# Batch 0 loaded nine rows to a partition, and weights in rows of 4 KB: a change to the start of an attention and FFN kernel

## The chip, the cores and the metric

The kernel runs on one core of a Trainium2 chip. TensorE (PE) multiplies; its weight loads (PEld) run beside its matmuls. VectorE (DVE), ScalarE (ACT) and GpSimd (POOL) work on elements. SyncE (SP) does no arithmetic here: its queue issues the DMA transfers, which 16 DMA engines carry out. The metric is the device time of one execution in microseconds; less is better.

## The reference

There are 8 batches of 8 heads, 576 rows and 64 columns a head. Only the largest scores of a row count, those within tau of its maximum; then a bilinear FFN follows.

```python
scores = scale * np.matmul(q, k.transpose(0, 1, 3, 2))
thresh = np.max(scores, axis=-1, keepdims=True) - tau
scores = np.where(scores >= thresh, scores, -1000000000.0)
scores = scores - np.max(scores, axis=-1, keepdims=True)
attn = np.exp(scores)
attn = attn / (np.sum(attn, axis=-1, keepdims=True) + 1e-09)
attn_out = np.matmul(attn, v)                 # (8, 8, 576, 64)
x = attn_out.transpose(0, 2, 1, 3).reshape(4608, 512)
out = ((x @ w_a) * (x @ w_b)) @ w_out         # w_a, w_b: 512x1536, w_out: 1536x512
```

q, k, v are float32. The three weights arrive as float64, so an element has 8 bytes; 512 x 1536 of them are 6.3 MB. The order of the keys within a head does not matter to the result as long as k and v have the same one; the order of the queries decides only which row of the output a result belongs to.

## The kernel before, in words

**Units and slots.** Two heads make a pair (index `i`, four pairs a batch). A unit `(i, u)` is 128 query rows of both heads of a pair (64 and 64 on the partitions), or the 64 rows that remain of two pairs. The main loop over `g` (L1000) takes one unit a slot and interleaves several stages: the scores of unit `g` on PE (L397, 16 recorded matmuls), its row maxima on DVE (L404), exponential on ACT (L425), threshold and row sums on DVE (L428), then the turned weights of earlier units times v (`product`, L535, tile pv). Matmuls are 64x64 and use the four quarters of the array side by side.

**Two ways to turn.** The first eight units (`BY_PE`) turn their attention weights on PE, by a product with a diagonal matrix (L472). Later ones are turned in blocks of 32 by DVE (L491), written to DRAM (`swap`, L497) and read back (`wT`, L514); for these, v has to lie in an order that fits the blocks. That is why `load_v` is called again for batch 0 in slots 8 to 11 (L1099).

**First rows.** q and k of batch 0 are loaded straight into "rooms" (L197): parts of tiles that are not yet in use, 96 partitions, six rows of 64 elements on each. `prep_pe` (L366) transposes them on PE, six transposes of 96 rows a matrix; `prep_copy` (L381) copies the result to SBUF on DVE, or ACT for the first k (L978). Pair 0 is prepared ahead of the loop, pair `g`+1 in slot `g`: q after the scores, k near the slot's end.

**Weights.** 36 pieces of [128, 512] are loaded by `load_weights` (L253) as raw float64 and made float32 by integer arithmetic: ACT takes the two halves of each number (L297, L298), POOL clamps (L304), DVE sets the sign and shifts (L310, L318), POOL adds (L323). A slot converts two pieces, slots 4 to 9 three. `load_weights` is called in four places of a slot and loads at most one piece at each, if a raw buffer or one of the idle tiles in `extra` is free; an issue then waits for the last PE instruction recorded ahead of it. Pieces 0 to 23 are w_a and w_b in turn, by column group of 512 columns: each is two transfers of 64 partitions with two runs of 2 KB. Pieces 24 to 35 are w_out, one transfer of 512 KB in runs of 4 KB.

**The FFN as a filler.** `ffn` is a generator of PE steps; `advance` (L910) takes steps out of it at several places of a slot until the columns owed are worked off. A step that is not ready (weights not converted, or rows of x not there) yields 0, and the advance is over. The first block (256 rows of batch 0) starts while weights are still being converted: six column blocks `f`, two to a column group, with 128 rows at a time for the first four of them (L758), then 256 rows. By the end of slot 4 the first 128 rows of x are there, by slot 9 all 256.

**Queues.** All instructions of an engine keep the order in which they are recorded. SP's transfers do too, and each waits for the completion of the transfer issued eight before it. PSUM is four double banks, shared by scores, transposes, pv, and the FFN.

Of the kernel before, what the change touches and what calls it, by code (L numbers as in the profile page):

```python
# [54 lines left out]
def kernel(  # L55
# [50 lines left out]
    R = 96  # L106
    NR = S // R
# [84 lines left out]
    def load_rows(i, name, room, engine=nc.sync):  # L192

        b, hp = pairs[i]
        for j in range(2):
            rows = {"q": q, "k": k}[name][b, 2 * hp + j]
            engine.dma_start(room[:, :, j * D:(j + 1) * D], rows.rearrange("(n p) d -> p n d", p=R))  # L197
        loaded.setdefault(i, {})[name] = room

    def load_v(i, again=False):  # L200
# [3 lines left out]
        for j in range(2):  # L204
            rows, half = v[b, 2 * hp + j], loaded[i]["v"][j * D:(j + 1) * D]
            if i >= HP or again:
                if i < HP:
                    rows = rows.rearrange("(c s p) d -> p c s d", c=2, p=Q)
                else:
                    rows = rows.rearrange("(p c s) d -> p c s d", c=2, p=Q)  # L210
                post(("v", i), *((half[c * Q:(c + 1) * Q], rows[:, c]) for c in range(2)))
            else:
                nc.sync.dma_start(half, rows.rearrange("(s p) d -> p s d", p=D))
# [11 lines left out]
    for f in range(NG):  # L225
        for c in range(HP):
            for dst, w in ((wa_sb, w_a), (wb_sb, w_b)):
                src = []
                for r in range(2):
                    chunks = [(2 * c + e) % HP * 2 + (r + (c >= HP // 2)) % 2 for e in range(2)]  # L230
                    cols = slice(f * CW + r * CH, f * CW + (r + 1) * CH)
                    rows = w[:, cols].bitcast(U32).rearrange("(k p) f -> p k f", p=D)
                    src.append(rows[:, chunks[0]:chunks[1] + 1:2])
                pieces.append((dst[:, f, 2 * c:2 * c + 2].rearrange("p k f -> p (k f)"), src))
    for F in range(NF):
        pieces.append((wo_sb[:, F, :], [w_out[F * P:(F + 1) * P, :].bitcast(U32)]))
# [42 lines left out]
    def convert_first(n):  # L279
# [17 lines left out]
        nc.scalar.activation(top, raw[:, :, 1].bitcast(FP32), AF.Abs)  # L297
# [22 lines left out]
    def convert_add(n):  # L320
        if n in stages:
            top, low = pieces[n][0].bitcast(I32), stages.pop(n).bitcast(I32)
# [6 lines left out]
    ROWS = 2 * NR * D  # L329
    rooms = []  # L330
    for _ in range(TW_BUFS):
        t = work.tile([P, 2 * NB, Q], FP32, tag="tw", bufs=TW_BUFS, name="rows")
        rooms.append(t.rearrange("p n e -> p (n e)")[0:R, 0:ROWS])
    rooms += [sums_sb[0:R, c:c + ROWS] for c in range(0, 5 * ROWS, ROWS)]
    rooms = [t.rearrange("p (n w) -> p n w", n=NR) for t in rooms]
# [30 lines left out]
    def prep_pe(i, name):  # L366

        m = loaded[i][name]
        if name == "q":
            mT = first_sb[:, i * S:(i + 1) * S]  # L370
        else:
# [788 lines left out]
```

## Time and profile before

| | |
|---|---|
| median of 3 runs | 1430.45 us (1425.97 to 1431.11) |
| the profiled execution | 1424.12 us, its span 1422.3 us |
| PE busy | 1370.2 us (96%) |
| DVE, ACT, POOL busy | 1005.4, 679.4, 480.9 us |
| DMA | 223.25 MB, 327003 packets, 171536 of them under 512 B |
| chain that ended last | PE 86%, DVE 8%, DMA 3%, issue 2% |

The span is the time from the first to the last instruction of the profiled execution; its own time is 1.8 us more. A group of instructions is given as line, engine, operation, output from input, shape and count. "Idle before" is time in which the engine stood still before the group, with what ended it; "issue" means that the profile shows nothing that it waited for. A share of the DMA engines above 1 comes from transfers that overlap in an engine. fp32 matmuls are recorded twice, transposes once.

### The profile page before, as it was taken

What the parts mean: (1) busy time and instruction counts of PE and PEld (TensorE: products, weight loads), DVE (VectorE), ACT (ScalarE), POOL (GpSimd) and SP (SyncE); (2) the same over time, 40 slices, a digit from 0 to 9 for tenths busy, and PEclk for the clock granted to TensorE, in tenths of its full rate; (3) what the DMA queues carried; (4) which work ended last, traced back from release to release, by engine and by line L of the source; (5) the groups of instructions that cost most, each with busy time, mean ns of one, the idle gap of its engine ahead of it and who ended that gap; (6) DMA issues with size and microseconds to landing.
All of it is one profiled execution on the core that took longest, in us unless ns stands there. A gap on an engine that the chain in (4) does not pass through costs nothing.

```text
span 1422.3 us, 76965 instructions
## 1 busy us (share of the span) xinstructions
PE 1370.2 (96%) x34208; PEld 1237.5 (87%) x34208; DVE 1005.4 (71%) x2196; ACT 679.4 (48%) x1244; POOL 480.9 (34%) x668
## 2 busy tenths in 40 slices
PE   6788999999999999999999999999999999999998
PEld 4677679999878897889999999988898999799998
DVE  6898876788677777786767767677767776744323
ACT  5877554545444554545444545454545545431010
POOL 2764541606060605133333324241515060605000
PEclk9989999999999999999999999999999999999999
DMA  9977786667656775667555766567655775550000
GB/s 211 235 210 202 179 218 161 178 159 194 172 144 167 190 195 147 178 160 185 143 131 151 179 178 168 138 161 212 159 145 145 209 182 152 130 151 18 3 18 17
DMA packets 327003, 223.25 MB, mean 157 GB/s; under 512 B 171536, under 2 KB 310800, under 8 KB 326672
## 3 DMA queue, kind: packets, MB, share of 16 engines
q1 hardware_dynamic: 324160, 217.74, 59.7%
q8 instruction: 269, 4.41, 1.3%
q10 hardware_dynamic: 2512, 0.59, 0.2%
q14 instruction: 62, 0.51, 0.1%
HBM read 128.58 MB, written 89.65 MB: 153 GB/s over the span
## 4 chain that ended last, share of the span: by engine, by line
PE 86%; DVE 8%; DMA 3%; issue 2%; ACT 1%; SPq 1%; DVEq 0%; ACTq 0%
PE pab L700 27%; PE po L830 20%; PE pab L773 18%; PE pv L535 10%; PE sc L397 9%; DVE mx L404 2%; DVE tw L491 1%; DVE tw L428 1%; SPq L143 1%; DMA wT<-swap 1%; DVE thr L405 1%; DVE low L310 1%; DMA more_u<-in_moe_w_a_dram 1%; PE tp L472 0%; DMA raw<-in_moe_w_b_dram 0%
## 5 line engine op out<-in xcount | busy, mean ns | idle before, releaser
L404 DVE TENSOR_REDUCE mx<-sc 128x1 f32<-128x576 f32 x288 | 204.6, 752 | 131.8 <-PE sc L397 131.4
L447 ACT ACTIVATE tw<-tw,rcp 128x576 f32<-128x576 f32 x272 | 196.1, 768 | 196.2 <-DVE rcp L441 196.1
L425 ACT ACTIVATE tw<-sc,bias,scalars 128x576 f32<-128x576 f32 x288 | 239.6, 832 | 10.9 <-PE pab L773 0.4
L666 POOL TENSOR_TENSOR h<-h,u 128x512 f32<-128x512 f32 x28 | 35.2, 1279 | 604.5 <-DVE h L743 428.0
L428 DVE SCALAR_TENSOR_TENSOR tw<-sc,thr,tw 128x576 f32<-128x576 f32 x288 | 221.2, 798 | 9.1 <-ACT tw L425 8.3
L830 PE MATMUL po<-wo_sb,h 64*64 64x256 f32 x3264 | 206.9, 376 | 1.2 <-DVE h L743 1.1
L491 DVE STREAM_TRANSPOSE tw<-tw 128x576 f32<-128x576 f32 x272 | 194.4, 752 | 0.8 <-ACT tw L447 0.8
L830 PEld LDWEIGHTS po<-wo_sb,h 64*64 64x64 f32 x3264 | 158.0, 133 | 25.6 <-DVE h L743 2.6
L535 PE MATMUL pv<-wT,vm 64*64 64x160 f32 (+3 forms) x5184 | 169.8, 273 | 7.0 <-DMA wT<-swap 2.4
L535 PEld LDWEIGHTS pv<-wT,vm 64*64 64x64 f32 x5184 | 159.3, 135 | 19.6 <-issue 9.6
L397 PE MATMUL sc<-kT,qT 64*64 64x288 f32 x2016 | 167.8, 404 | 0.6 <-DVE xT L543 0.3
L830 PE MATMUL po<-sums_u,h 64*64 64x256 f32 x2448 | 154.1, 376 | 0.5 <-DVE h L781 0.5
L799 POOL TENSOR_TENSOR h<-h 128x256 f32<-128x256 f32 x168 | 117.5, 734 | 106.5 <-PE po L830 101.7
L830 PEld LDWEIGHTS po<-sums_u,h 64*64 64x64 f32 x2448 | 117.6, 133 | 20.3 <-DVE h L781 1.6
L700 PE MATMUL pab<-xU,wb_sb 64*64 64x128 f32 x4096 | 131.6, 269 | 0.0
L700 PEld LDWEIGHTS pab<-xU,wb_sb 64*64 64x64 f32 x4096 | 126.9, 133 | 2.6 <-ACT h L725 0.5
L397 PEld LDWEIGHTS sc<-kT,qT 64*64 64x64 f32 x2016 | 102.5, 133 | 20.8 <-issue 4.6
L542 ACT COPY xT<-pv 128x128 f32<-128x128 f32 (+1 forms) x68 | 17.6, 259 | 206.5 <-PE pv L535 206.5
L424 ACT ACTIVATE bias<-mx,scalars 128x1 f32<-128x1 f32 x288 | 82.7, 287 | 68.3 <-DVE mx L404 68.0
L543 DVE COPY xT<-pv 64x128 f32<-64x128 f32 (+1 forms) x136 | 38.1, 281 | 92.3 <-PE pv L535 91.1
L773 PE MATMUL pab<-xS,wa_sb 64*64 64x256 f32 (+1 forms) x1536 | 98.8, 361 | 0.0
L773 PE MATMUL pab<-xS,wb_sb 64*64 64x256 f32 (+1 forms) x1536 | 97.0, 360 | 0.7 <-issue 0.7
(136 smaller groups left out, 2370.1 us busy)
## 6 DMA issues: line engine op xcount, KB each, us to landing
wT<-swap SPq DMA_DIRECT2D x244, 288.0 KB, 4.0
swap<-tw SPq DMA_DIRECT2D x480, 144.0 KB, 3.1
vm<-in_v_dram SPq DMA_DIRECT2D x128, 72.0 KB, 2.5
swap<-tw SPq DMA_DIRECT2D x128, 72.0 KB, 3.2
kT<-in_k_dram SPq DMA_DIRECT2D x112, 72.0 KB, 3.4
wT<-swap SPq DMA_DIRECT2D x56, 144.0 KB, 3.6
out_dram<-kept SPq DMA_DIRECT2D x30, 256.0 KB, 3.8
qT<-in_q_dram SPq DMA_DIRECT2D x112, 40.0 KB, 3.0
```

What stands on the lines that cost most here:

```text
L397: nc.tensor.matmul(sc[m][o * D:(o + 1) * D, c], qT[r, q0:q0 + D], kT[r, c * SH:(c + 1) * SH], start=True, stop=True)
L404: nc.vector.tensor_reduce(mx[:, c], sc[j], axis=AX.XY, op=ALU.max)
L424: nc.scalar.activation(bias[:, j:j + 1], mx[:, j:j + 1], AF.Copy, scale=e_nscale)
L425: nc.scalar.activation(wb[j], sb[j], AF.Exp, bias=bias[:, j:j + 1], scale=e_scale)
L428: nc.vector.scalar_tensor_tensor(out=wv, in0=sb[j], scalar=thr[:, j:j + 1], in1=wv, op0=ALU.is_ge, op1=ALU.mult, accum_out=sums[:, j:j + 1])
L447: nc.scalar.activation(w, w, AF.Copy, scale=rcp[:, j:j + 1])
L491: nc.vector.transpose(w, w)
L535: nc.tensor.matmul(pv[c * D:(c + 1) * D, y], vm[rows, s], wT[y](rows, s), start=(s == 0), stop=(s == NSLOT - 1))
L700: nc.tensor.matmul(out[c * D:(c + 1) * D, r, f * P:(f + 1) * P], w[g][k][rows, w0:w0 + D], moving[k][rows], start=(fresh and k == 0 and f ...
L773: nc.tensor.matmul(pab[c * D:(c + 1) * D, r], w[rows, f // n, k, fs + c * D:fs + (c + 1) * D], moving, start=(k == 0), stop=(k == H - 1))
L799: (nc.vector if state["over"] else nc.gpsimd).tensor_tensor(*a, **kw)
L830: nc.tensor.matmul(po[c * D:(c + 1) * D, r, y], ht[rows, t0:t0 + D], other[rows, f], start=(f == 0), stop=(f == NF // 2 - 1))
```

## The change

- q and k of batch 0: partition p of 64 takes nine rows that follow each other in DRAM (2304 B), q of a pair on the lower and k on the upper 64 partitions of one room. Keys and queries of batch 0 are thereby in another order: row 9p + n of the head is entry 64n + p.
- `prep_pe` transposes with matmuls of 64x64 against the identity, 20 a matrix (slot 4 of the nine is cut in two where a PSUM bank ends), q and k of pair 0 in one interleaved run.
- v of batch 0 is loaded in the same order, 2304 B to a partition; when it is loaded again for the blocks, in 8 transfers a pair instead of 4.
- The output rows of batch 0 are written back in their order: [2, 64 rows] instead of [128 rows] a transfer.
- Weights: column group 0 as before. Groups 1 and 2 come together: all pieces of w_a, then of w_b, each in two transfers of 64 partitions with one run of 512 columns (4 KB); half of the array's rows works on columns 512 to 1023, the other half on 1024 to 1535. The rows of w_out are permuted to fit.
- The first block therefore has 128 rows at a time only for the first two column blocks, then 256 rows: w_a for the rest, then w_b. Its steps wait for 8, 16 and 24 converted pieces.
- One of the four places of a slot that load a weight piece is gone.

```diff
@@ load_rows, load_v
-            engine.dma_start(room[:, :, j * D:(j + 1) * D], rows.rearrange("(n p) d -> p n d", p=R))
+            engine.dma_start(room[:, j], rows.rearrange("(p n) d -> p (n d)", p=D))
...
-                    rows = rows.rearrange("(c s p) d -> p c s d", c=2, p=Q)
+                    rows = rows.rearrange("(x p n) d -> p x n d", x=2, p=Q)
+                    post(("v", i), *((half[c * Q:(c + 1) * Q, y::2],
+                                      rows[:, (c + y) % 2, (c * NSLOT + y) // 2:(c * NSLOT + y) // 2 + (NSLOT + 1 - y) // 2])
+                                     for c in range(2) for y in range(2)))
...
-                nc.sync.dma_start(half, rows.rearrange("(s p) d -> p s d", p=D))
+                nc.sync.dma_start(half, rows.rearrange("(p s) d -> p s d", p=D))
@@ weight pieces
-    for f in range(NG):
-        for c in range(HP):
-            for dst, w in ((wa_sb, w_a), (wb_sb, w_b)):
...
+    for c in range(HP):
+        for dst, w in ((wa_sb, w_a), (wb_sb, w_b)):
...
+            pieces.append((dst[:, 0, 2 * c:2 * c + 2], src))
+    for dst, w in ((wa_sb, w_a), (wb_sb, w_b)):
+        for c in range(H):
+            src = []
+            for r in range(2):
+                rows = w[chunk_of(c, r) * D:(chunk_of(c, r) + 1) * D, CW + r * CW:2 * CW + r * CW]
+                src.append(rows.bitcast(U32).rearrange("p (k f) -> p k f", k=2))
+            pieces.append((dst[:, 1:NG, c], src))
     for F in range(NF):
-        pieces.append((wo_sb[:, F, :], [w_out[F * P:(F + 1) * P, :].bitcast(U32)]))
+        g, r, y = F // NT, F // 2 % 2, F % 2
+        row = (F if g == 0 else NT + r * NT + (g - 1) * 2 + y) * P
+        pieces.append((wo_sb[:, F, :].rearrange("p (k f) -> p k f", k=2), [w_out[row:row + P, :].bitcast(U32)]))
@@ prep_pe
-                nc.tensor.transpose(tp[:, c, n * R:(n + 1) * R], m[:, c * (NR // 2) + n], ident[0:R, 0:R])
...
+        for n in range(NSLOT):
+            for c0, c1 in ((0, D),) if n != NT else ((0, Q), (Q, D)):
+                c, to = divmod(n * D + c0, SH)
+                for name, (_, tp) in zip(names, both):
+                    m, r = loaded[i][name], "qk".index(name) * D
+                    for j in range(2):
+                        nc.tensor.matmul(tp[j * D:(j + 1) * D, c, to:to + c1 - c0], m[:, j, n * D:(n + 1) * D],
+                                         ident[r:r + D, r + c0:r + c1], start=True, stop=True)
@@ ffn
-            steps = [(f, c, c + P) for c in (0, P) for f in range(2 * n)] + steps[2 * n:]
+            steps = ([(f, c, c + P, both) for c in (0, P) for f in range(n)]
+                     + [(f, 0, HALF, (w,)) for w in both for f in range(n, NG * n)])
...
-                while (state["converted"] < 2 * HP * (f // n + 1)
+                while (state["converted"] < 2 * HP * (1 + (f // n > 0) * (1 + any(w is wb_sb for w in both)))
@@ rows_out
-            pending.append((out[r0:r0 + P, :], t))
+            to = out[r0:r0 + P, :]
+            if b == 0:
+                n = (h * HALF + u * P) // D
+                to = out[0:S, :].rearrange("(p n) d -> n p d", n=NSLOT)[n:n + 2]
+            pending.append((to, t))
@@ main loop
-        load_weights(RAWS, most=1)
         if here:
             weigh(i, u)
```

## The prediction

> **What bounds the kernel now.** I read the page's parts 1 and 2 first, then the busy time by stage, then the order of time on TensorE, VectorE and the DMA queue inside the stage that is not full.
>
> The stages (columns: stretch in us, its length, then PE, PEld, DVE, ACT and POOL busy us with instruction counts, granted clock, DMA share, GB/s):
>
> ```profile
> 0.00:60.00 60.00, 39.17 (x796) 31.28 (x796) 44.89 (x107) 40.39 (x83) 27.71 (x39) 0.97 1.11 225
> 60.00:100.00 40.00, 34.26 (x930) 31.93 (x934) 35.04 (x75) 32.14 (x64) 27.69 (x32) 0.87 0.72 191
> 100.00:185.00 85.00, 74.68 (x1597) 58.55 (x1593) 74.64 (x167) 54.11 (x105) 40.74 (x40) 0.96 0.78 203
> 185.00:1285.00 1100.00, 1090.55 (x27586) 987.14 (x27582) 802.81 (x1762) 537.84 (x970) 366.99 (x531) 1.00 0.64 166
> 1285.00:1422.30 137.30, 131.52 (x3322) 128.61 (x3314) 47.99 (x88) 14.94 (x24) 17.79 (x29) 0.99 0.05 15
> ```
>
> From 185 us on PE is busy 99% and 96% of the time. The instruction order of the two kernels on PE is the same from the second FFN block on, apart from a few groups of 4 matmuls that change sides of a scores group. So the change can move the end only through the first 185 us, where PE idles 20.8 + 5.7 + 10.3 = 36.9 us. The end moves with the time at which the first block is through (before: 185 us, in slot 21).
>
> In that stage the work goes slot by slot: scores, row maximum, exponential, threshold, and two or three weight pieces converted. By the starts of the row maxima a slot lasts 7.2, 7.4, 7.9, 6.6, 7.1, 9.1, 12.2, 9.3, 11.3 and 9.8 us (slots 0 to 9). DVE is busy for nearly all of a 7 us slot; ACT, with three pieces, for about 8.4 us. Slots 6 and 8 stand out. The order of time on PE, then on DVE, says why (start, duration, group; in brackets the idle time before it and what ended it):
>
> ```profile
> 5.33 2.15 PE L376 MATMUL tp<-more_u,rows 96*128 96x96 f32 x12 [5.33 <-DMA rows<-in_q_dram]
> ...
> 53.83 1.22 PE L397 MATMUL sc<-kT,first_u 64*64 64x288 f32 x15
> 58.10 0.40 PE L397 MATMUL sc<-kT,first_u 64*64 64x288 f32 x1 [3.06 <-issue]
> ...
> 60.20 3.85 PE L472 MATMUL tp<-first_u,tw 128*64 128x128 f32 x36 [0.65 <-DVE xT L543]
> ...
> 81.66 1.99 PE L773 MATMUL pab<-xT,wa_sb 64*64 64x128 f32 x32 [1.45 <-DVE tw L428]
> 83.39 1.96 PE L773 MATMUL pab<-xS,wa_sb 64*64 64x128 f32 x32
> 85.10 1.96 PE L773 MATMUL pab<-xT,wb_sb 64*64 64x128 f32 x32
> ```
>
> ```profile
> 58.54 0.76 DVE L404 TENSOR_REDUCE mx<-sc 128x1 f32<-128x576 f32 x1 [2.14 <-PE sc L397]
> ...
> 88.37 1.42 DVE L404 TENSOR_REDUCE mx<-sc 128x1 f32<-128x576 f32 x2 [2.60 <-PE sc L397]
> ```
>
> In slot 6 PE stopped for 3.06 us before the last of 16 scores matmuls with nothing that the profile shows to wait for: the instruction itself was late, while the DMA engines were full (share 1.07). The 36 matmuls after it then took 3.85 us instead of 2.19, at a granted clock of 0.66. In slot 8 a filler of 96 first-block matmuls ran at half rate (1.96 us a group instead of 1.08), the next scores stood behind it, and DVE idled 2.60 us.
>
> No converting instruction waits for a weight transfer in this stage: the waits list a DMA only for the first rows (5.3 us) and 0.2 us for v. Weights are issued early enough to hide a landing of 7 to 8 us. So faster weight transfers, by themselves, are worth nothing on the chain.
>
> **The change part by part.** Gains are negative.
>
> *First rows.* q and k of pair 0 (590 KB) go as 64 runs of 2304 B a transfer instead of 576 of 256 B. The first landing ended at 5.19. The engines moved 265 to 275 GB/s at their best between 2.5 and 4 us, and 337 from 105 to 110 us, when w_out's rows of 4 KB were in flight. 590 KB at 270 is 2.2 us, at 337 1.75. I take 0.7 us, bounds 0 and 1.5.
>
> *Transposes.* Per matrix six full-width transposes (0.71 us warm, 1.22 cold) become 20 matmuls of 64x64, which the profile will count as 40, as it counts 16 for 8 scores matmuls. The nearest row is pv with 72 such on four quarters in 1.27 us: 18 to a quarter, 70 ns each. Pair 0 uses all four quarters: 20 x 70 = 1.4 us warm, 2.1 to 2.4 at the cold rate (the first scores took 2.2 us instead of 1.2), against 2.15 before. Nothing. Pairs 1 to 3 have two quarters only: 1.07 to 1.4 warm, about 2.1 cold, so +0.4 to +0.9 each, six times. For k DVE comes 0.5 us later anyway and covers some; for q the copy is what DVE does next. I put 0.55 + 0.55 + 0.5 = +1.6 over slots 0 to 2, bounds 0 (PE idles 6 us there) and +4.
>
> A rule of the Trainium skill bears on this. TensorEngine Tiling (Array Packing), "Restrictions", says that column tiling rules out the transpose mode for FP32 input; TensorE: Matmul & The Clock Gate calls that mode four times as fast for FP32 under "Terms". By the rule a matrix would take 4 x 0.71 / 2 = 1.4 us, the upper of my two warm values, and the term would be near +2.5.
>
> *Slot 6.* Rows of 2304 B and 4 KB instead of 256 B and 2 KB, and at most three pieces a slot instead of four, take the DMA engines off their limit (share 1.06 to 1.29 from 5 to 65 us). If the 3.06 us was an instruction fetch behind full queues, it goes, and DVE is late next: -3.0, to the 9.1 us of its neighbours. Bounds 0 (it stays, or comes elsewhere) and -3.7.
>
> *Slot 8.* The first block now has only column group 0 to work on until w_a of both other groups is converted and both row halves are there, in slot 9. The 96 matmuls of slot 8 move to slots 9 to 20. Slot 8 falls to its ACT work, 8.6 us: -2.7. Of the moved 2.6 us of PE, 1.1 us each come into slots 10 and 11, where PE idles 1.6 and 1.4 us but not always when filler is at hand: +0.7, between 0 and 2.6. By the order, the first block is through in slot 21 in both. Together -2.0, bounds +2.6 (slot 8 stays and the work is pure extra) and -2.7.
>
> *SP in slots 8 to 12.* v of batch 0 is loaded again with 8 transfers a pair instead of 4: 16 more issues, median 0.454 us each, 7.3 us. SP is the queue to look at here (start, time taken, group):
>
> ```profile
> 113.21 4.28 SPq L143 DMA_DIRECT2D swap<-tw  x8
> 118.33 1.81 SPq L143 DMA_DIRECT2D vm<-in_v_dram  x4
> 120.24 3.27 SPq L143 DMA_DIRECT2D swap<-tw  x4
> 123.62 1.08 SPq L143 DMA_DIRECT2D wT<-swap  x2
> ```
>
> From 87 to 134 us SP issues for 36.5 of 47 us. The last line's two transfers feed the pv matmuls at 127.77, which PE reached 1.85 us early. Four more v issues (1.8) and one more w_out transfer (0.35) and its wait stand ahead of them: +2.5. Bounds 0, if less loaded engines finish sooner (each transfer of SP waits for the one issued eight before it), and +7.3, all of the issues.
>
> *Stores of batch 0.* Four transfers [128 rows] become [2, 64 rows], 2 KB runs as before. Stores of 256 KB landed in 3.8 us (longest 5.2) and nobody waited: 0.
>
> The Trainium skill, DMA: Bandwidth & Descriptors, "Why a DMA increments its semaphore by 16 and not by 1", speaks against it: the slowest dimension sets how many engines share a transfer, here 2. At the 426 GB/s that all 16 reached at best, two move 256 KB in 4.9 us, and the swap reads behind them come as much later; the sum would be 1 to 3 us higher. No row of before shows such a store.
>
> *Conversion.* The same 36 pieces with the same element counts on ACT, DVE and POOL, top written as two runs of 256: 0, with bounds -1 and +1 from the spread of one shift (0.41 to 1.5 us beside POOL's adds). Nothing would cover more: DVE and ACT are nearly full in these slots.
>
> **Sum.** -0.7 + 1.6 - 3.0 - 2.0 + 2.5 = -1.6 us. Against the profiled execution (span 1422.3, 1424.1 in all) that is 1422.5. That execution lay 6.3 us below the median of the runs, 1430.45; taken off the median, 1428.8, and I say 1429. Of this kernel a measurement can tell about 0.5% (7.2 us) from no change.
>
> **The rivals.**
> 1. *The holes close and the costs hide* (faster). First rows -1.5, transposes 0, slot 6 -3.7, slot 8 -2.7, pv no longer waiting -1.9: -9.8, 1420.7. For it: PE idles 36.9 us in the stage and DVE's own work would fit shorter slots. Against it: SP's load grows where it is already 78% busy.
> 2. *SP becomes the bound in slots 9 to 13* (slower). All 7.3 us of issues delay the swap reads, the fillers behind pv wait too, and slots 10 to 13 lengthen; with the transposes at +4 and slot 6 and 8 giving -3, +8.3: 1438.8. Without SP's term the sum is -4.1, so it decides from 4.1 us of delay on, 0.26 us for each of the 16 issues. For it: the back-to-back issues above, in order, each behind DVE's transposes. Against: 10 us of gaps between 87 and 134.
> 3. *The transfers were hidden anyway.* The 3.06 us stop is tied to where the instruction stream is cut, not to full queues, and returns elsewhere (another of 1.2 us stands at 1100 and later with a share of 0.6). Then +1.4: 1431.9, no change.
>
> **How the numbers follow.** Forecast 0.38, rival 3 0.16, rival 1 0.26, rival 2 0.20. Rival 1 and rival 2 end past the bound of 7.2 us, the forecast and rival 3 within it: faster 0.26, slower 0.20, same 0.54. The range of 8 in 10 reaches from rival 1 with 2 us of run spread (1419) to rival 2 (1439). The forecast's own range is 1424 to 1434.
>
> **What would show it.** Right: q and k landing before 5 us; six transposing groups of 40 at over 1 us; no PE stop near 55 us and DMA share under 1 by then; no first-block matmuls in slot 8, and that slot under 9 us; pv of slot 13 waiting 3 us or more; the first block through a few us before 185. Wrong: a converting instruction on ACT that waits for a weight transfer, since third pieces are now issued about one slot ahead; a stop for instructions of 3 us elsewhere; wT reads landing 5 us late behind the stores; or any difference after 200 us.

## The result: 1.3% slower

| | before | after |
|---|---|---|
| median (beside each other on one chip) | 1429.89 us (1425.77 to 1431.11, 6 runs) | 1445.49 us (1443.89 to 1452.27, 6 runs) |
| ratio, 95% interval | | 1.0127 [1.0099, 1.0155] |
| both again on another chip | 1426.24 us (27 runs) | 1444.82 us (6 runs); ratio 1.0133 [1.009, 1.0176] |
| the profiled execution, its span | 1424.12, 1422.3 us | 1452.27, 1450.5 us; the second one 1439.13, 1437.3 us |
| DMA packets | 327003 | 312867 |

The forecast was 1429 us, "no change", with a range that ended at 1439. The kernel is 15.6 us slower beside before on the first chip and 18.6 on the second. The first profile of after is of the slowest of its six runs, the second profile of the fastest of its six, so the two lie on either side of the median.

The stages of the profile after, with the columns as before (stretch in us, its length, busy time and instruction count of PE, PEld, DVE, ACT and POOL, granted clock, DMA share, GB/s):

```profile
0.00:60.00 60.00, 46.48 (x990) 39.56 (x994) 42.46 (x102) 38.72 (x79) 24.88 (x36) 0.86 0.86 210
60.00:100.00 40.00, 31.77 (x900) 27.68 (x896) 39.03 (x80) 34.09 (x70) 31.25 (x36) 0.96 0.72 193
100.00:185.00 85.00, 71.81 (x1308) 53.90 (x1304) 70.06 (x147) 48.34 (x93) 38.70 (x37) 0.94 0.74 194
185.00:1285.00 1100.00, 1078.27 (x26917) 964.73 (x26911) 803.20 (x1762) 539.28 (x969) 364.61 (x527) 0.99 0.64 165
```

What the change was to do for the DMA engines, it did: the share in the first 60 us falls from 1.11 to 0.86. What it did to the time is in the third row. From 100 to 185 us PE handles 1308 recorded matmuls where it handled 1597.

A better reading than PE's busy time is a ladder: the start of the row maximum of each slot, from the order of time on VectorE, less that of before. Where the difference grows, time is lost; where it shrinks, time is won.

| slot | before, us | after | after, second profile |
|---|---|---|---|
| 4 | 39.5 | +5.1 | +3.9 |
| 6 | 55.7 | +5.1 | +4.0 |
| 7 | 67.8 | +2.0 | +2.1 |
| 9 | 88.4 | -1.0 | -0.6 |
| 13 | 124.0 | -0.5 | +0.1 |
| 14 | 133.9 | +7.0 | +8.9 |
| 16 | 149.2 | +8.3 | +10.2 |
| 17 | 154.5 | +11.6 | +13.5 |
| 22 | 192.0 | +9.9 | +11.7 |
| 23 | 200.9 | +14.4 | +13.2 |
| 33 | 283.8 | +14.1 | +13.4 |
| 34 | 293.4 | +18.6 | +17.7 |
| 44 | 377.7 | +18.0 | +15.9 |
| 108 | 946.9 | +21.1 | +16.3 |
| 114 | 999.6 | +27.4 | +16.3 |

The steps that both profiles show are: the start (+4 to +5), the holes of slots 6 and 8 (-4.5 to -6), slot 13 to 14 (+7.5 and +8.8), slot 16 to 17 (+3.3), slot 22 to 23 (+4.5 and +1.5), slot 33 to 34 (+4.5 and +4.3). The +6.3 between slots 108 and 114 is in the first profile alone, an accident of that execution.

The order of time on PE shows the steps (start, duration, group; in brackets the idle time before it and what ended it):

```profile
5.51 2.40 PE L394 MATMUL tp<-more_u,rows 64*64 64x64 f32 x78 [0.88 <-DMA rows<-in_q_dram]
...
18.22 2.34 PE L394 MATMUL tp<-more_u,rows 64*64 64x64 f32 x40
20.50 4.11 PE L490 MATMUL tp<-first_u,tw 128*64 128x128 f32 x36
24.53 1.99 PE L394 MATMUL tp<-more_u,rows 64*64 64x64 f32 x40
...
59.44 1.22 PE L415 MATMUL sc<-kT,first_u 64*64 64x288 f32 x16 [0.33 <-issue]
...
134.30 4.07 PE L553 MATMUL pv<-wT,vm 64*64 64x32 f32 x144 [6.86 <-DMA wT<-swap]
...
209.58 3.32 PE L553 MATMUL pv<-wT,vm 64*64 64x128 f32 x67 [2.26 <-DMA wT<-swap]
...
305.89 4.30 PE L553 MATMUL pv<-wT,vm 64*64 64x160 f32 x69 [2.82 <-DMA wT<-swap]
```

The same places in before, the first three against the second to fourth line above:

```profile
17.57 1.22 PE L376 MATMUL tp<-more_u,sums_u 96*128 96x96 f32 x6
18.73 2.45 PE L472 MATMUL tp<-first_u,tw 128*64 128x128 f32 x36
21.69 0.71 PE L376 MATMUL tp<-more_u,sums_u 96*128 96x96 f32 x6 [0.52 <-DVE tw L428]
...
127.77 3.57 PE L535 MATMUL pv<-wT,vm 64*64 64x32 f32 x144 [1.85 <-DVE tw L491]
```

The first line of after is the whole of the first rows' profit: the bulk of pair 0's transposes begins at 5.51 us (6.32 in the second profile), where before all of them began at 5.33. The next three are the dearer start: a matrix takes 2.34 and 1.99 us where it took 1.22 and 0.71, and the turn between them 4.11 instead of 2.45. At 59.44 the stop of 3.06 us is gone. The last three are waits for the reading back of the turned weights. Before, the list of waits has that once, 2.4 us at 180 us; the 1.85 us ahead of slot 13's pv it puts down to a transposing instruction on VectorE. In after it says:

```profile
PE pv L553 <- DMA wT<-swap: 13.7, 4, 6.9
```

And this wait costs more than itself: the 144 matmuls behind the 6.86 us took 4.07 us, while in a run below (the second load of v moved away), behind a wait of 0.58 us, 143 of them took 2.29.

The step from slot 16 to 17 lies on VectorE, with GpSimd beside it. In after, VectorE first:

```profile
158.94 1.61 DVE L423 TENSOR_SCALAR thr<-mx,scalars 128x2 f32<-128x2 f32 x1
...
163.96 0.64 DVE L801 TENSOR_TENSOR h<-h,pab 128x512 f32<-128x512 f32 x1
164.53 1.53 DVE L457 TENSOR_SCALAR sums<-sums 128x2 f32<-128x2 f32 x1
```

```profile
158.69 3.61 POOL L667 TENSOR_TENSOR sums_u<-wo_sb 128x768 f32<-128x768 f32 x2
...
164.21 3.60 POOL L667 TENSOR_TENSOR sums_u<-wo_sb,sums_u 128x768 f32<-128x768 f32 x2
```

and the two small instructions in before:

```profile
150.65 0.23 DVE L405 TENSOR_SCALAR thr<-mx,scalars 128x2 f32<-128x2 f32 x1
...
154.28 0.15 DVE L439 TENSOR_SCALAR sums<-sums 128x2 f32<-128x2 f32 x1
```

They take 1.4 us more each, and with the multiply of 0.6 us that before does not have there this is the whole step. Each begins 0.2 to 0.4 us after the first of two adds on GpSimd, and ends within 0.1 us of that add's end.

### The profile page after: what moved, and what is told of

The parts are those of the page before. It is cut to its first block, busy times and chain, and to the rows that moved or that the text cites. A ratio compares the mean times of both kernels' runs of the same rounds, so it can differ in the third digit from the quotient of the medians.

```text
span 1450.5 us, 77012 instructions
## 1 busy us (share of the span) xinstructions
PE 1388.0 (96%) x34224; PEld 1245.0 (86%) x34224; DVE 1011.2 (70%) x2194; ACT 679.3 (47%) x1242; POOL 481.0 (33%) x668
## 2 busy tenths in 40 slices
DMA packets 312867, 223.25 MB, mean 154 GB/s; under 512 B 157912, under 2 KB 297176, under 8 KB 312536
## 4 chain that ended last, share of the span: by engine, by line
PE 83%; DVE 8%; DMA 5%; SPq 2%; issue 2%; ACT 0%; ACTq 0%; DVEq 0%
PE pab L718 26%; PE po L849 20%; PE pab L793 16%; PE pv L553 9%; PE sc L415 9%; DVE mx L422 2%; DMA wT<-swap 1%; SPq L141 1%; PE po L895 1%; DVE tw L446 1%; DVE tw L509 1%; DVE low L322 1%; DMA swap<-tw 1%; DVE wb_sb L330 0%; DMA raw<-in_moe_w_out_dram 0%
## 5 line engine op out<-in xcount | busy, mean ns | idle before, releaser
L443 ACT ACTIVATE tw<-sc,bias,scalars 128x576 f32<-128x576 f32 x288 | 239.6, 832 | 10.7 <-ACT bias L442 0.6
L553 PE MATMUL pv<-wT,vm 64*64 64x160 f32 (+3 forms) x5184 | 177.6, 280 | 17.0 <-DMA wT<-swap 13.7
L553 PEld LDWEIGHTS pv<-wT,vm 64*64 64x64 f32 x5184 | 166.6, 140 | 27.1 <-issue 17.0
L718 PE MATMUL pab<-xS,wa_sb 64*64 64x128 f32 x2048 | 100.2, 269 | 1.3 <-issue 1.3
```

What stands on the lines that cost most here:

```text
L443: nc.scalar.activation(wb[j], sb[j], AF.Exp, bias=bias[:, j:j + 1], scale=e_scale)
L553: nc.tensor.matmul(pv[c * D:(c + 1) * D, y], vm[rows, s], wT[y](rows, s), start=(s == 0), stop=(s == NSLOT - 1))
L718: nc.tensor.matmul(out[c * D:(c + 1) * D, r, f * P:(f + 1) * P], w[g][k][rows, w0:w0 + D], moving[k][rows], start=(fresh and k == 0 and f ...
```

## The experiments

All starts of row maxima below are given against the profile of before, as in the ladder.

### The stores: undone, and alone

Undone in the kernel after: every store of batch 0 as two transfers of 64 rows, with the order of the rows as it is.

```diff
-                to = out[0:S, :].rearrange("(p n) d -> n p d", n=NSLOT)[n:n + 2]
-            pending.append((to, t))
+                to = out[0:S, :].rearrange("(p n) d -> n p d", n=NSLOT)
+                pending.append(((to[n], t[0:D]), (to[n + 1], t[D:P])))
...
-            post("out", pending.pop(0))
+            post("out", *pending.pop(0))
```

> The changed kernel with the stores of batch 0 issued as two transfers of 64 rows each instead of one of [2, 64 rows]; all else as changed. Theory A (the stores go over two DMA engines, and the transposed weights behind them land late): the waits of pv on the read-back at 209 and 305 us (2.3 and 2.8 us, and the cold matmuls after them) go, swap writes land in 3.7 us again instead of 6.6 between 185 and 225 us, and the time falls by 7 to 10 us, to 1436 to 1438. Theory B (all of the loss is the queue of the reloads in slots 8 to 13, the later waits are its echo): both waits stay in some form and the time moves by less than 2 us.

Measured: 1438.29 us (1437.03 to 1438.49) against 1425.56, ratio 1.0097 [1.0077, 1.0118]. Slot 22 +10.8, 23 +11.1, 33 +10.7, 34 +10.5: both steps are gone, and slot 44 stands at +9.8 instead of +18.0. The wait in slot 13 stays. In the times the gain is less sure than in the ladder: the interval of this ratio overlaps that of the kernel after, 1.0127 [1.0099, 1.0155].

Alone, in the kernel before, first try: the same rows to the same place with the shape [2, 64 rows].

```diff
+            if b == 0:
+                to = to.rearrange("(n p) d -> n p d", n=2)
             pending.append((to, t))
```

> Before, with nothing but the shape of the stores of batch 0: the same 128 rows to the same place, written as [2, 64 rows] instead of [128 rows]. Theory (the outer dimension of 2 lets only two of the 16 DMA engines carry a store, and the swap transfers behind it on these engines come late): steps of 4 to 5 us between slots 22 and 23 and between 33 and 34, the median landing of swap transfers at 185 to 225 us near 6.6 us instead of 3.7, slot 44 at +8 to +9 us, ratio 1.0055 to 1.0065. Rival (the stores hurt only because the kernel after runs late there): under 2 us in each place, ratio below 1.002.

Measured: 1426.13 us against 1426.24, ratio 0.9992 [0.9967, 1.0017]. The stores landed in 3.2 us, slots 22 and 23 stand at +2.5 and +2.5, slots 33 and 34 at +2.4 and +2.3. It looks like the rival, but the run doesn't test it: half n, row p goes to row 64n + p, so that the two dimensions are one in memory. The second try keeps them apart. Partition p of half n goes to row 2p + n, so the output rows of batch 0 stand in another order than the reference has them; the work is the same:

```diff
-                to = to.rearrange("(n p) d -> n p d", n=2)
+                to = to.rearrange("(p n) d -> n p d", n=2)
```

> Before, with nothing but the stores of batch 0 as [2, 64 rows] whose two dimensions can't be joined: partition p of half n goes to row 2p + n of the block, in runs of 2 KB as before (the rows of batch 0 thus stand in another order within their blocks of 128; all work is done). In the run before, partition n * 64 + p went to row n * 64 + p, so that the two dimensions are one in memory and the transfer could be the old one: its stores landed in 3.2 us and no step was seen. Theory (an outer dimension of 2 that stays puts a store on two DMA engines): no landing of a store is shown within 16 engines, swap transfers at 185 to 225 us land in about 6 us instead of 3.7, steps of 1.5 to 5 us come between slots 22 and 23 and between 33 and 34, slot 44 at +6 to +9 us, ratio 1.004 to 1.0065. Rival (it is the stride of nine rows in DRAM, or the late state of the queue in the kernel after): steps under 1 us, landing near 3.7 us, ratio below 1.002.

Measured: 1435.52 us against 1427.36, ratio 1.0053 [1.0027, 1.0079]. Slot 22 +2.5, 23 +7.6, 33 +7.9, 34 +12.3: steps of 5.2 and 4.4 us. The DMA issues of this run from 180 to 220 us (KB each, then the median us from issue to landing):

```profile
swap<-tw SPq DMA_DIRECT2D x20, 144.0 KB, 7.0
...
out_dram<-osb SPq DMA_DIRECT2D x2, 256.0 KB
```

and of before in the same stretch:

```profile
swap<-tw SPq DMA_DIRECT2D x20, 144.0 KB, 3.7
...
out_dram<-osb SPq DMA_DIRECT2D x2, 256.0 KB, 3.8
```

The bytes, the 2 KB runs and the number of transfers are the same. The store in the first fence has no landing, because the view counts a transfer as landed when all 16 engines have reported it, and here not all of them carried it. What it costs is in the other line: the swap transfers behind it take 7.0 us instead of 3.7. A stride of nine rows isn't needed for it, nor a late queue.

The semaphore updates that the trace holds count the engines. In before each of the four stores of batch 0 has 16 updates, between 2.9 and 5.2 us after its issue. In this run each has three: one at 1.0 us, and two at 7.6 to 8.9 us, or at 12.7 to 12.8 for the second of two stores that follow each other at once. The kernel after has the same pattern of three, and the first try, whose dimensions merge, has 16. The update at 1.0 us is earlier than any of the 16 in the other stores (1.95 us at the least), so two engines carry the data. This is what the rule says that the prediction quoted from the Trainium skill (DMA: Bandwidth & Descriptors, "Why a DMA increments its semaphore by 16 and not by 1").

### The second load of v: moved away, and alone

In the kernel after, the second load of v of pairs 2 and 3 in slots 13 and 14 instead of 10 and 11, still in 8 transfers a pair:

```diff
+RELOAD = [8, 9, 13, 14]
...
-        if BY_PE <= g < BY_PE + HP:
-            load_v(g - BY_PE, again=True)
+        if g in RELOAD:
+            load_v(RELOAD.index(g), again=True)
```

> The changed kernel with the second load of v for pairs 2 and 3 (16 of its 32 transfers) in slots 13 and 14 instead of 10 and 11; all else as changed. Theory B (SP's queue is the bound in slots 10 to 13): the wait of pv in slot 13, 6.9 us in the changed kernel and 1.9 before, falls to 3 us or less, slot 13 loses its 7.5 us, and the time falls by 5 to 8 us, to 1438 to 1440. Theory A (two-engine stores carry the loss): the wait in slot 13 falls, but the filler there only moves, and the time falls by less than 2 us.

Measured: 1436.38 us (1434.79 to 1443.56) against 1425.56, ratio 1.0096 [1.0063, 1.0128]. Slot 13 -0.3, slot 14 -1.1: the loss of 7.5 us is not there. The steps of the stores stay (slot 22 +1.7, 23 +4.6, 33 +4.3, 34 +7.4). SP's queue shows why. The kernel after (start, time that the queue took, group):

```profile
108.02 6.66 SPq L141 DMA_DIRECT2D vm<-in_v_dram  x8
114.72 0.95 SPq L141 DMA_DIRECT2D wT<-swap  x2
115.77 0.41 SPq L282 DMA_DIRECT2D more_u<-in_moe_w_out_dram  x1
116.28 5.77 SPq L141 DMA_DIRECT2D swap<-tw  x8
122.14 0.38 SPq L282 DMA_DIRECT2D more_u<-in_moe_w_out_dram  x1
122.63 0.40 SPq L282 DMA_DIRECT2D sums_u<-in_moe_w_out_dram  x1
123.07 5.00 SPq L141 DMA_DIRECT2D vm<-in_v_dram  x8
128.17 1.82 SPq L141 DMA_DIRECT2D swap<-tw  x4
130.09 1.08 SPq L141 DMA_DIRECT2D wT<-swap  x2
```

and with the two loads moved:

```profile
111.68 5.76 SPq L142 DMA_DIRECT2D swap<-tw  x8
117.54 0.93 SPq L283 DMA_DIRECT2D more_u<-in_moe_w_out_dram  x1
118.57 0.38 SPq L283 DMA_DIRECT2D sums_u<-in_moe_w_out_dram  x1
119.03 2.23 SPq L142 DMA_DIRECT2D swap<-tw  x4
121.36 1.80 SPq L142 DMA_DIRECT2D wT<-swap  x2
128.09 1.78 SPq L142 DMA_DIRECT2D swap<-tw  x4
```

The two reads that feed pv in slot 13 (last line of the first fence, fifth of the second) are issued at 130.09 and at 121.36. In the first the queue has no gap from 108 us on: 16 issues of v took 6.66 + 5.00 us, 0.83 and 0.63 each, not the 0.45 that the prediction took from the median. (Before had shown it: of its four groups of four v issues from 87 us on, three took 2.68 to 3.23 us, 0.67 to 0.81 an issue; the prediction showed only the fourth, 1.81.) In the second the queue rests 5 us before 128.09.

Alone, in the kernel before, its own second load cut into 8 transfers a pair, with the same bytes in the same slots:

```diff
...
+                    post(("v", i), *((half[c * Q:(c + 1) * Q, y::2], rows[:, c, y::2])
+                                     for c in range(2) for y in range(2)))
...
```

> Before, with nothing but the second load of v of batch 0 cut finer: 8 transfers a pair instead of 4, in the same slots 8 to 11 and with the same bytes and runs of 256 B. Theory (the issues themselves, some 0.45 us each in SP's queue, make the reading back late): pv of slot 13 waits 5 to 9 us for wT instead of 1.85, slot 14 starts 4 to 8 us late, and the end is as much late, ratio 1.003 to 1.006. Rival (it was the other order of the rows, or the weights' transfers, that delayed the queue): slot 14 within 1.5 us, ratio 1.000.

Measured: 1433.98 us against 1426.24, ratio 1.0043 [1.0018, 1.0068]. Slot 12 0.0, 13 +4.6, 14 +10.8, 44 +10.7. PE's order of time:

```profile
121.74 4.02 PE L539 MATMUL pv<-wT,vm 64*64 64x128 f32 x67 [3.06 <-DMA wT<-swap]
...
136.84 4.07 PE L539 MATMUL pv<-wT,vm 64*64 64x32 f32 x144 [5.54 <-DMA wT<-swap]
```

So the number of issues alone is enough. The waits add up to 8.6 us, and both groups behind them ran slow; the shift in the profile is somewhat larger than expected, the time is in the range.

### Both undone

The two edits together in the kernel after.

> The kernel after, with both earlier edits together: each batch-0 store as two transfers of 64 rows, and the second v load of pairs 2 and 3 in slots 13 and 14. Theory (two separate losses that add up): the ratios alone were 1.0097 and 1.0096 against 1.0127 of the kernel after, so together 1.0066, between 1.003 and 1.008; by the starts of the row maxima, slot 14 within 1 us of before, slot 44 at about +2.5, with only the late start (+5 us by slot 4) and +3.3 us between slots 16 and 17 left. Rival (one loss hides behind the other, the queue being late in either case): no better than each alone, 1.009 or more, and a new wait of pv for wT of 4 us or more somewhere between slots 22 and 34.

Measured: 1430.64 us against 1426.31, ratio 1.0023 [1.0002, 1.0043]. Slot 9 -1.5, 14 -2.0, 17 +2.6, 22 +0.9, 34 +0.6, 44 -0.8. In the ladder at slot 44 the stores were worth 8.2 us, the loads 11.2, both together 18.8. In the ladder they add up, and together they are the loss of the kernel after but for about 0.2%. In the times they do more than add up: each alone had brought the ratio from 1.0127 to 1.0096 or 1.0097, which gave the expected 1.0066, and the 1.0023 lies below the expected range. The two runs alone had four executions each, and their intervals are too wide to say which of the two sums is right.

### The start: wider transposes, and the turning alone

In the kernel after, the two heads of a pair interleaved in the room (runs of 256 B again) so that one transpose of 64x128 does what two matmuls did:

```diff
-            engine.dma_start(room[:, j], rows.rearrange("(p n) d -> p (n d)", p=D))
+            engine.dma_start(room[:, :, j], rows.rearrange("(p n) d -> p n d", p=D))
...
-                    for j in range(2):
-                        nc.tensor.matmul(tp[j * D:(j + 1) * D, c, to:to + c1 - c0], m[:, j, n * D:(n + 1) * D],
-                                         ident[r:r + D, r + c0:r + c1], start=True, stop=True)
+                    nc.tensor.transpose(tp[:, c, to:to + c1 - c0], m[c0:c1, n].rearrange("p j d -> p (j d)"),
+                                        ident[r + c0:r + c1, r + c0:r + c1])
```

> The changed kernel with q and k of a pair beside each other in the room (runs of 256 B on the SBUF side) and transposed by 10 transposes of 64 rows by 128 columns a matrix instead of 20 matmuls of 64x64; all else as changed. Theory C (the narrow matmuls cost the 4 to 5 us that slots 1 to 4 are late): slot 4 starts 3 to 4 us earlier than in the changed kernel (row maximum at 41 us instead of 44.6) and the time falls by 3 to 4 us, to 1442. Rival (the lateness comes from the landing of the first rows, or from PE at half clock whatever it does): slot 4 stays within 1 us of 44.6 us and the time does not move, or it is later because the first rows land later in short runs.

Measured: 1445.28 us (1443.78 to 1450.53) against 1425.56, ratio 1.0157 [1.0124, 1.019]; slot 4 +6.9, later still. The lines say that several things moved against each other:

```profile
6.93 1.64 PE L393 MATMUL tp<-more_u,rows 64*128 64x64 f32 x20 [6.93 <-DMA rows<-in_q_dram]
...
19.06 1.54 PE L393 MATMUL tp<-more_u,rows 64*128 64x64 f32 x10
...
24.57 1.55 PE L393 MATMUL tp<-more_u,rows 64*128 64x64 f32 x10
27.05 2.21 PE L414 MATMUL sc<-kT,first_u 64*64 64x288 f32 x16 [0.94 <-ACT first_u L472]
...
32.60 3.89 PE L489 MATMUL tp<-first_u,tw 128*64 128x128 f32 x36
36.41 1.03 PE L393 MATMUL tp<-more_u,sums_u 64*128 64x64 f32 x10
```

The turning got cheaper (1.55 and 1.03 us against 2.0 to 2.3 and 1.38), and the first rows were there at 6.93 us, against 5.51 and 6.32 in the two profiles of the kernel after. PE also stayed slow for longer: the scores at 27 us took 2.21 us and the turn at 32.6 us 3.89, where the kernel after took 1.22 and 2.19. That costs about as much between slots 2 and 3 (+2.3 us, against +1.0 in after) as the cheaper turning saves. This run can't price the parts, so the turning was changed alone, in the kernel before, with rows and loads as they were:

```diff
-                nc.tensor.transpose(tp[:, c, n * R:(n + 1) * R], m[:, c * (NR // 2) + n], ident[0:R, 0:R])
+                for j in range(2):
+                    nc.tensor.matmul(tp[j * D:(j + 1) * D, c, n * R:(n + 1) * R],
+                                     m[:, c * (NR // 2) + n, j * D:(j + 1) * D], ident[0:R, 0:R], start=True, stop=True)
```

> Before, with one thing changed: q and k of batch 0 are turned by plain matmuls against the identity, 12 of 96x64 a matrix, in place of 6 transposes of 96x128; rows, layout and loads stay. Theory (the +5 us of the start is the dearer turning itself, and the lower clock that it meets): a turned matrix takes 1.2 to 2.5 us instead of 0.7 to 1.2, the row maximum of slot 4 starts 3 to 5 us late, and with nothing that gives it back the end is 3 to 5 us late, ratio 1.002 to 1.0035. Rival (the start is late because of the new loads, or the number of instructions, 40 recorded a matrix): slot 4 within 1 us of before, ratio 1.000.

Measured: 1431.41 us against 1426.31, ratio 1.0028 [1.0008, 1.0048]. Slot 2 +2.9, 4 +8.0, 9 +3.4, 33 +4.3. A matrix took 2.1 to 2.2 us cold and 1.21 warm; slot 4 is later than expected because a stop of 2.90 us for an instruction fell into slot 2 here, and less of one into slot 6. The end is in the range: the dearer turning alone costs about 4 us of time (0.28%). Part of slot 4's +8.0 is the stop, which in before stands in slot 6.

### The holes: the weights alone, then without the queue behind them

In the kernel before, the weights' part of the change alone: the pieces, the steps of the first block, three places.

```diff
+    for dst, w in ((wa_sb, w_a), (wb_sb, w_b)):
+        for c in range(H):
...
+            pieces.append((dst[:, 1:NG, c], src))
...
+            steps = ([(f, c, c + P, both) for c in (0, P) for f in range(n)]
+                     + [(f, 0, HALF, (w,)) for w in both for f in range(n, NG * n)])
...
-        load_weights(RAWS, most=1)
         if here:
             weigh(i, u)
```

> The kernel before with only the weights part of the change: rows of 4 KB for column groups 1 and 2, the new order of the first block's steps and three places a slot. q, k, v and the stores of batch 0 as before. Theory D (the two long slots close by this part): the stop of 3.06 us at 55 us and the cold filler of slot 8 go, slot 9 starts 5 to 6 us earlier than before (row maximum at 82 to 83 us instead of 88.4), slots 10 and 11 give 1 us back, and the time falls by 3 to 5 us, to 1425 to 1427. Rival (the stop is tied to where the instruction stream is cut): a stop of 2 us or more stays in slots 5 to 8 and the time stays within 2 us of before.

Measured: 1427.01 us against 1425.56, ratio 1.0007 [0.9986, 1.0029]. Slot 9 -3.7, 13 -5.3: the gain is there. Slot 14 -0.6, 17 +4.0, 44 +0.6: it is gone one slot later, where PE waits 4.34 us for wT. The stop in slot 6 is gone here, but stops of 1.09, 1.94 and 1.74 us for an instruction stand at 37, 44 and 51 us instead. The slots ahead had become faster; the reading back had not, because the queue paces it. So the same with the second load of v in slots 13 and 14:

> Before, with the weights' part of the change alone (layout, steps, three places), as in the run that came out at 1.0007, and the second v load of pairs 2 and 3 in slots 13 and 14. Theory (the reading back of wT through SP's queue is what took the gain of the closed holes away): slot 13 stays at -5 us and slot 14 is now at -5 us as well instead of -0.6; of that 3 us are lost again by slot 17, and the end is at -2 to -4 us, ratio 0.997 to 0.9985; the wait of pv for wT in slot 13 falls from 4.3 us to under 1 us. Rival (the blocks are ready on VectorE too late for an earlier slot 13, whatever the queue does): the wait keeps 3 us or more, slot 14 at -1, ratio 1.000.

Measured: 1424.16 us against 1426.31, ratio 0.9987 [0.9971, 1.0004]. PE's order of time shows no wait of pv for wT up to 345 us, and slot 13 (-2.1) passes its lead on to 14 (-3.0). But the lead was smaller this time, since PE had stopped for 3.88 us in slot 6, and 3.3 us were lost from slot 16 to 17: 44 stands at -2.0. That move by itself, in the kernel before:

> Before, with nothing but the second v load of pairs 2 and 3 in slots 13 and 14. Theory (in the kernel before, the queue is at its limit in slot 13 already, by the 1.85 us that PE waited there): that wait goes, slot 14 at -1 to -2 us, ratio 0.9985 to 0.9995. Rival (in the kernel before, the row work sets the pace of these slots, and the reading back is only just in time): no difference, ratio 1.000, slot 14 within 0.5 us. If the loads are merely moved into a place that is as tight, slot 14 to 17 are later by 1 to 2 us, ratio 1.001.

Measured: 1427.12 us against 1426.31, ratio 1.0006 [0.9979, 1.0034], slot 14 -0.9, 17 +0.9, 22 +0.1. The wait in slot 13 did not go (2.40 us). This is the rival, no difference: in the kernel before the reading back is just in time, and there is no lead that it could hold up.

The run before this one, with the new weights and the moved loads, has the same instructions up to slot 10 as the run of the weights alone, and in it the stop in slot 6 was there (3.88 us). So the new weights by themselves do not remove it. In the last variant of this line, built on that run, slots 0 to 3 load a weight piece in two places instead of three:

```diff
-        load_weights(RAWS, most=1)
+        if g >= 4:
+            load_weights(RAWS, most=1)
```

> The best version so far (before, with the weights' part of the change and the second v load of pairs 2 and 3 in slots 13 and 14), and in slots 0 to 3 only two of the three places load a weight piece. Theory (PE's stop of 3 to 4 us for an instruction fetch comes from DMA engines that are full from 25 to 60 us): the DMA share from 25 to 45 us falls from 1.12 to about 0.9, no stop above 1.5 us is left ahead of 65 us, slot 7 at -1 to -2 us against before instead of +2.5; what of it reaches the end is 0 to 3 us, ratio 0.9965 to 0.9985. Rival 1 (the stop belongs to the place in the instruction stream): it stays at 3 us or more near 55 us whatever the share. Rival 2 (weights then land too late): ACT waits for raw in slots 4 to 9 for several us, ratio above 1.000.

Measured: 1424.44 us against 1426.24, ratio 0.9968 [0.9944, 0.9991] (the two medians alone would give 0.9987). Slot 7 -2.2, 13 -5.4, 14 -4.7, 17 -0.1, 44 -3.3. The ratio sets it below 1; the median is the same as without this edit (1424.16), so that the edit itself gains is not shown. PE's order of time without the edit:

```profile
51.80 1.08 PE L787 MATMUL pab<-xS,wa_sb 64*64 64x128 f32 x32
...
53.55 1.22 PE L409 MATMUL sc<-kT,first_u 64*64 64x288 f32 x15
58.65 0.63 PE L409 MATMUL sc<-kT,first_u 64*64 64x288 f32 x1 [3.88 <-issue]
```

and with it:

```profile
52.66 2.01 PE L787 MATMUL pab<-xS,wa_sb 64*64 64x128 f32 x32
...
55.59 1.22 PE L409 MATMUL sc<-kT,first_u 64*64 64x288 f32 x15
57.05 0.40 PE L409 MATMUL sc<-kT,first_u 64*64 64x288 f32 x1 [0.23 <-issue]
```

PE's instructions are the same in both, so the place in the stream alone does not make the stop. Two things differ. One packet of 16 KB on the instruction queue begins at 55.97 us without the edit and at 54.54 with it. And PE reaches the last of the 16 matmuls 2.0 us later with it (56.81 instead of 54.77), because the 96 matmuls of filler ahead took 1.68, 2.01 and 1.43 us a group, behind an idle 1.33 us, and 1.10, 1.08 and 1.08 without it, behind 0.79. Together that is nearly all of the 3.65 us by which the stop is shorter.

From the begin of the packet to the instruction it took 2.68 us without the edit and 2.51 with it. The same holds elsewhere: behind 29 stops of 0.3 us or more in the first 76 us of all the profiles, before's 3.06 us among them, PE goes on 2.5 to 3.0 us after such a packet began, at DMA shares of 0.41 to 1.22 in between. So a full set of DMA engines does not make the fetch itself longer. What sets the length of a stop is how early the packet begins against how far PE has come.

Why it begins when it does, no run here shows. Full engines may hold it back: from 54 to 56 us the share was 1.09 in before and 1.08 without the edit, where the stops were 3.1 and 3.9 us, and 0.49 with it. But it was 1.08 in the run of the weights alone too, where these matmuls had no stop. In none of the six profiles with the whole change or most of it (the kernel after twice, and its four variants) is a stop above 0.4 us left ahead of 76 us; all the other profiles have one of 1.5 us or more. Which part of the change does that was not tested.

The expected fall of the share was not there: from 25 to 45 us it stayed at 1.12, and from 45 to 65 us it was 0.83, against 0.86 without the edit. Stops of 1.5 and 1.7 us appeared after 65 us.

### The kernel after once more

> The kernel after once more, unchanged, beside before on this chip. Theory (the ladder of losses read in its first profile is that of the kernel, but for the last step): start +5 us by slot 4, holes -6 us by slot 9, +7.5 us from slot 13 to 14, +4.5 us from 22 to 23 and from 33 to 34, slot 44 at +18 us; the +6 us between slots 108 and 114 belongs to the one execution and is not seen again; ratio 1.0115 to 1.014. Rival (the steps are accidents of that execution): other places, other sizes.

Measured: 1444.82 us against 1426.24, ratio 1.0133 [1.009, 1.0176]; the second column of the ladder above. All steps came back in their places, with sizes that differ by 1.5 us at most, but for the stores at slot 22 (1.5 instead of 4.5); the one between slots 108 and 114 did not.

## Why the prediction was wrong

It named every part of the change that moved the time, and was right on the sizes of the two holes and of the conversion. Its sum failed by three sizes: the start, SP's queue and the stores. And one premise was wrong: that the change could move the end only through the first 185 us. The stores of batch 0 lie behind that, and cost the kernel 6 to 9 us there.

- **First rows** (-0.7): nothing gained. The rows that PE needs were there at 5.51 and 6.32 us in the two profiles, against 5.33 before. The estimate was made from the bytes and the best rates, and the landing did not follow them.
- **Transposes** (+1.6, up to 4): +4 to +5, counting what lies behind them. The warm price was right (1.38 us against the 1.4 of the upper end). The cold price of 2.1 us was right too (2.0 to 2.3). What failed is how much of it was counted: 1.6 us for six matrices, where in the first profile their PE time grew from 5.74 to 10.05 us, and nothing for the turn between them (4.11 for 2.45). "Nothing" for pair 0 was 0.6 us (its copy to SBUF started at 7.94 instead of 6.56). The rule weighed here (TensorEngine Tiling (Array Packing), "Restrictions") pointed to the dearer side, which was right; the turning alone cost about 4 us.
- **Slot 6** (-3.0): -3.1 and -1.9 in the two profiles of after. That it was an instruction fetch is borne out: PE went on 2.6 us after a packet of 16 KB began. That full DMA engines were the cause is not shown; the fetch took as long at half the share.
- **Slot 8** (-2.0): -2.7 in both. But the deferred work cost +3.3 from slot 16 to 17, not +0.7. The step is in every profile with the new weights (3.3 or 3.4 us) and absent in three of the five variants with the old ones, while two of them, the later load and the merging stores, have 1.7 us of it, one such instruction. Of the 3.3 us, 0.6 is the deferred multiply on VectorE; the rest is two small VectorE instructions that end only with an add on GpSimd (the lines above). That the adds fall on them because of the deferred work was not tested, and stays open.
- **SP in slots 8 to 12** (+2.5): +7.5 and +8.8. This is rival 2, and its condition, "from 4.1 us of delay on", was met. The failed step is to count only the four v issues just ahead of the last wT read: from 92 us on the queue has no gap above 0.3 us, 12 of the 16 added issues are in that row, and an issue behind others costs 0.6 to 0.8 us, not the median of 0.454. The price of 7.3 was the right bound by accident; the group behind the wait ran slow on top.
- **Stores** (0, or 1 to 3 by the page): +9 in the first profile, +6 in the second, +9.6 alone in the ladder (ratio 1.0053). This was no rival at all. "Nobody waited" was true of the old stores and says nothing about those behind a store of another shape. The page's rule was at hand and right in kind; the estimate made from it took one delay of 4.9 us as partly hidden. A store took 7.8 us or more to land on its two engines, and at two places the chain of swap, wT and pv came late behind one.
- **Conversion** (0): right. The waits of the first 110 us in the profile after list a DMA only for the first rows.

The forecast's sum set gains in slots 6 and 8 against costs later as if they were paid in one currency. They are not: the weights alone gained 5.3 us up to slot 13, and the next wait took all but 0.6. A gain ahead of a queue that is just in time is worth what the queue lets through. With the sizes of the first profile in its places the sum is 0 + 5.1 - 3.1 - 2.7 + 3.3 + 7.5 + 9.0 = +19.1 us; the ladder has +18.0 at slot 44, and the medians differ by 15.6 and 18.6. The parts alone in the kernel before (stores 0.53%, issues of v 0.43%, turning 0.28%, weights 0.07%) add up to 1.31%, against 1.27% and 1.33% for the whole; this is an estimate, since the stores alone had another stride.

## What to carry to other kernels

Cut or reorder a transfer only after reading the queue that issues it: when it issues without a gap, every added transfer delays the read at the end of that queue by 0.6 to 0.8 us, and moving two loads by three slots was worth 11 us in the ladder, and 0.3% (stores as changed) to 0.7% (stores undone) of the time. Keep partitions as the one outer dimension of a store; nobody waited for the four 256 KB stores as [2, 64 rows] themselves, but alone they cost 4 to 5 us at each of two places behind them. And look for what is late next behind a hole before pricing the hole: here closing both was worth nothing until the loads of v were moved too, and then 0.1%, within the noise, to 0.3%.

The best version found is the kernel before with the new weights, the two v loads in slots 13 and 14, and fewer weight pieces in slots 0 to 3: 0.9968 [0.9944, 0.9991].

## What the runs showed of the hardware that was not expected

- A [2, 64 rows] store of 256 KB whose dimensions stay apart is carried by two engines (three semaphore updates instead of 16), lands in 7.8 us or more, and nearly doubles the landing of the transfers behind it (3.7 to 7.0 us for 144 KB); one whose dimensions merge in memory has 16 updates, lands in 3.2 us and is harmless.
- PE goes on 2.5 to 3.0 us after a 16 KB packet on the instruction queue begins, behind all 29 stops looked at, at DMA shares from 0.41 to 1.22.
- Idle time on PE can be followed by slow matmuls. Behind waits of 4.3, 4.9, 5.5, 6.9 and 8.5 us the 144 pv matmuls of slot 13 took 4.06 or 4.07 us each time; behind 0.6 us 143 took 2.29. For shorter waits there is no such rule here: behind 1.85 us in before they took 3.57, behind 2.2 and 2.4 us in two variants 142 took 2.76 and 3.18.
- Two VectorE instructions of 0.15 and 0.23 us took 1.5 to 1.6 us where an add on GpSimd had just begun, and ended with it: 2.7 us of the chain in every profile with the new weights.
